# First batch's q and k loaded in rows of 2 KB and set beside each other on chip, with the planner's numbers anew

## The chip, the cores and the metric

The kernel runs on one core of a Trainium2 chip. The metric is the device time of one execution in microseconds (us); less is better. The engines named below are PE (TensorE, with its weight loads PEld), DVE (VectorE), ACT (ScalarE), POOL (GpSimd) and SP (SyncE, here the one queue that issues all DMAs).

## What is computed

Dilated and plain windowed attention over 4 batches, 8 heads, 576 tokens and 64 numbers a head, then two gated MLPs over the 2304 tokens. Cut to what matters:

```python
scores = scale * np.matmul(q, k.transpose(0, 1, 3, 2))        # q, k, v: (4, 8, 576, 64) float32
masks = [mask_plain if h < H // 2 else mask_dil for h in range(H)]   # 32 keys; or 32 keys at distance 4
attn = softmax(np.where(masks, scores, -1e9))
x = np.matmul(attn, v).transpose(0, 2, 1, 3).reshape(2304, 512)
xn = x / rms(x) * rms_g                                       # first MLP; weights are float64
x = (silu(xn @ w_gate) * (xn @ w_val)) @ w_out                # d_ff = 1536
return (sigmoid(x @ w2_gate) * (x @ w2_val)) @ w2_out         # second MLP
```

## The kernel before

**Work and order.** No engine's order is written by hand. Every piece of work is entered by `add(engine, cost, fn, reads, writes, tiles, due, other)`; `Line.emit` then runs a list scheduler that gives each engine the piece that can start first by modelled costs, ties by `due`. `other` names another engine that may take the piece, with a penalty from the table `PARAMS`. The table also holds the due times of attention groups, loads, weights and stores. What comes out is a fixed order on each of PE, DVE, ACT, POOL and SP; each engine works its list off in order, and so does SP's DMA queue.

**Attention.** Heads go in pairs `hp` (0 and 1 plain, 2 and 3 dilated), queries in blocks of 64, three blocks to a group: 4 batches x 4 pairs x 3 groups. A group (`attn_group`) is: scores on PE (L943), mask and maximum on DVE (L955), three exponentials on ACT (L961), a reciprocal on DVE (L968, L969), scaling on POOL (L974, or DVE L978, ACT L981), a transposition on PE (L988), a copy out of the bank (L993), the product with the values on PE (L1001) and a copy into the tile `xT` (L1013 or L1021).

**Loads of the first batch.** `first_qk` (L763) loads k and q of one head pair of batch 0 into a raw tile of 72 partitions: partition p holds eight tokens of both heads, token by token, so that PE can transpose both heads of a token row at once (L796, eight transpositions of 72x128, in two banks of four). Copies out of the banks (L807) put them in the order in which the attention reads them. The raw tiles lie in the rings `xo` (pairs 2 and 3), `pt` (pair 0) and `wo` (pair 1). The whole of that load is one DMA of 1152 rows of 256 bytes:

```python
raw = new(pool_, ring, [TP, 8, 2, D], F32, bufs)              # TP = 72, D = 64
out=raw.t, in_=src[b, 2*hp:2*hp+2].rearrange("e (p n) d -> p n e d", n=8)
```

Values of batch 0 come by `first_v` (dilated, tile `xT`, L855) and `values_of`. The other batches are loaded by `attn_load` (L902, rows of 128 bytes) and transposed by DVE (L916).

**MLPs.** The 2304 tokens go in six chunks of 384. `x_norm` squares x on ACT (L1051), sums on PE (L1067), takes the inverse root on DVE (chunk 0) or POOL, spreads it by PE (L1124) and writes `xn` on DVE (L1147). Every operand is split in a high and a low part by `split`: high by ACT (L582) or DVE (L584), low = source - high by POOL (L586) or DVE (L589). A step (chunk c, slice f of d_ff) is g and v (L1362, 12 matmuls each), the gate (ACT L1404, DVE L1406, L1410), the split of `h`, and one step later y (L1442, 12 matmuls). First-MLP weights are float64 bits: `words` makes float32 of one 128-row slice by ACT (L563) and four DVE instructions (L566, L569, L572, L575), behind a load of 512 KB (L542, L546) into the ring `wst` of three. The second MLP works with 2x2 block products (L1670, L1593) from about 600 us on.

## Time and profile before

| | |
|---|---|
| median of 3 runs | 1005.12 us (1004.35 to 1007.39) |
| the profiled execution | 1005.76 us, of which the span from first to last instruction is 1004.0 us |
| PE busy in the span | 974.6 us (97%), mean granted clock 0.979 |
| DVE, ACT, POOL busy | 732.4 (73%), 478.3 (48%), 405.8 (40%) us |
| DMA packets | 213252, of them 137312 under 512 B |
| DMA, mean over the span | 194 GB/s |

PE's time splits in two. From about 255 us on it is busy practically without a gap until 983 us. Before that lie the starting stage, up to the first product of the MLP, and a stage in which attention of later batches and steps of the first MLP are mixed. A stretch of the trace shows what an engine lost in two ways: as time in which it was not busy, and as granted clock below 1.00 (the clock has two levels, 1.2 and 2.4 GHz; 0.80 is a mean over the stretch). Durations given for one instruction overlap a little with the next one, so the distance between starts is the better price.

### The profile page before, as it was taken

How to read it: one execution, taken by the hardware profiler on the slowest of the kernel's cores; microseconds unless marked ns; L12 is line 12 of the kernel's file. 1: busy time of each engine (PE TensorE's matmuls, PEld its weight loads, DVE VectorE, ACT ScalarE, POOL GpSimd, SP SyncE). 2: the span in 40 equal slices, each digit the busy share in tenths (PEclk: the TensorE clock that was granted, in tenths of full speed). 3: DMA queues.
4: the chain of work that ended last, by engine and by line, in shares of the span. 5: the costliest groups of instructions: out<-in, count | busy, mean ns of one | idle time of the engine just before them, and what ended most of it. 6: DMA issues, size and time to landing. Idle time of an engine off the chain costs nothing. (4 is left out here: it accounts for less than half of the span.)

```text
span 1004.0 us, 20084 instructions
## 1 busy us (share of the span) xinstructions
PE 974.6 (97%) x7096; PEld 946.2 (94%) x7096; DVE 732.4 (73%) x1712; ACT 478.3 (48%) x1305; POOL 405.8 (40%) x602
## 2 busy tenths in 40 slices
PE   7898899999999999999999999999999999999997
PEld 6678798998999999999999999999999999999996
DVE  6787897867886888744432569778977688788766
ACT  5976657646432443222221336546654455454432
POOL 5663874443433640010000457337753037661111
PEclk8789799999999999999999999999999999999999
DMA  8858698676779687974662455545276463547634
GB/s 205 191 148 179 134 288 222 155 214 183 236 232 311 228 278 240 331 252 176 234 220 88 136 162 190 210 183 173 69 259 212 156 225 124 189 151 236 161 79 93
DMA packets 213252, 194.53 MB, mean 194 GB/s; under 512 B 137312, under 2 KB 178848, under 8 KB 213152
## 3 DMA queue, kind: packets, MB, share of 16 engines
q1 hardware_dynamic: 213152, 193.25, 63.5%
q8 instruction: 56, 0.92, 0.4%
q14 instruction: 44, 0.36, 0.1%
HBM read 129.50 MB, written 63.70 MB: 192 GB/s over the span
## 5 line engine op out<-in xcount | busy, mean ns | idle before, releaser
L1442 PE MATMUL y<-h,wo 128*128 128x384 f32 x864 | 167.9, 340 | 0.5 <-DVE h L589 0.4
L1362 PE MATMUL g<-xo,w 128*128 128x384 f32 x864 | 165.7, 340 | 0.0
L1362 PE MATMUL v<-xo,w 128*128 128x384 f32 x864 | 162.9, 336 | 0.0
L1442 PEld LDWEIGHTS y<-h,wo 128*128 128x128 f32 x864 | 150.5, 189 | 2.5 <-DVE h L589 0.7
L1362 PEld LDWEIGHTS g<-xo,w 128*128 128x128 f32 x864 | 152.2, 191 | 0.3
L1362 PEld LDWEIGHTS v<-xo,w 128*128 128x128 f32 x864 | 150.2, 188 | 1.3
L582 ACT CAST h<-t 128x384 fp32r<-128x384 f32 (+1 forms) x139 | 65.7, 473 | 111.9 <-DVE t L1410 86.3
L586 POOL TENSOR_TENSOR h<-t,h 128x288 fp32r<-128x288 f32 (+1 forms) x45 | 42.0, 934 | 156.6 <-ACT h L582 151.2
L1410 DVE TENSOR_TENSOR t<-t,v 128x384 f32<-128x384 f32 x72 | 39.6, 550 | 64.0 <-PE v L1362 63.3
L1542 DVE SCALAR_TENSOR_TENSOR pt<-y,pt 128x288 f32<-128x288 f32 x133 | 60.0, 452 | 36.0 <-PE y L1593 33.3
L974 POOL TENSOR_SCALAR pr<-pr,rs 128x96 f32<-128x96 f32 x132 | 57.1, 446 | 56.3 <-DVE rs L969 44.0
L589 DVE TENSOR_TENSOR h<-t,h 128x384 fp32r<-128x384 f32 (+1 forms) x95 | 58.5, 616 | 24.9 <-ACT h L582 23.9
L1593 PE MATMUL y<-h,wo 128*128 128x288 f32 x399 | 72.7, 295 | 0.3 <-ACT h L582 0.2
L586 POOL TENSOR_TENSOR w<-wz,w 128x256 fp32r<-128x256 f32 x58 | 47.3, 830 | 48.5 <-ACT w L582 35.2
L563 ACT ACTIVATE wz<-wst 128x512 f32<-128x512 f32 x72 | 47.9, 669 | 35.1 <-DMA z<-wz 21.7
L1593 PEld LDWEIGHTS y<-h,wo 128*128 128x128 f32 x399 | 59.5, 188 | 0.8 <-ACT h L582 0.5
L586 POOL TENSOR_TENSOR w<-S,w 128x256 fp32r<-128x256 f32 x48 | 38.7, 820 | 52.2 <-DVE w L584 38.0
L572 DVE SCALAR_TENSOR_TENSOR wz<-wst,wz 128x512 int32<-128x512 int32 x72 | 55.8, 775 | 0.9
L961 ACT ACTIVATE pr<-pr,nmx 128x96 f32<-128x96 f32 x144 | 52.4, 366 | 8.0 <-DVE nmx L955 7.7
L575 DVE SCALAR_TENSOR_TENSOR wz<-wst,wz 128x512 int32<-128x512 int32 x72 | 53.2, 738 | 0.6
L1696 ACT ACTIVATE t<-t 128x288 f32<-128x288 f32 x72 | 31.9, 444 | 45.5 <-DVE t L1687 43.9
L586 POOL TENSOR_TENSOR x<-t,x 128x288 fp32r<-128x288 f32 x29 | 27.2, 942 | 64.3 <-ACT x L582 64.3
(231 smaller groups left out, 2112.8 us busy)
## 6 DMA issues: line engine op xcount, KB each, us to landing
z<-wz SPq DMA_DIRECT2D x54, 256.0 KB, 4.7
xo<-xs SPq DMA_DIRECT2D x23, 576.0 KB, 5.7
wst<-in_moe_w_gate_dram SPq DMA_DIRECT2D x24, 512.0 KB, 4.6
wst<-in_moe_w_val_dram SPq DMA_DIRECT2D x24, 512.0 KB, 5.4
wst<-in_moe_w_out_dram SPq DMA_DIRECT2D x24, 512.0 KB, 5.4
xs<-xs SPq DMA_DIRECT2D x21, 576.0 KB, 2.8
wst<-xs SPq DMA_DIRECT2D x18, 576.0 KB, 5.3
x<-xo SPq DMA_DIRECT2D x24, 384.0 KB, 3.2
```

The source lines that it names most:

```text
L563: add("ACT", act(CW), lambda: nc.scalar.activation(out=z.t.bitcast(F32), in_=top().bitcast(F32), func=ACTF.Abs), reads=[("wst", key)], wri ...
L572: add("DVE", Shared(0.595), lambda: nc.vector.scalar_tensor_tensor(out=z.t, in0=top(), scalar=-0x40000000, in1=z.t, op0=ALU.bitwise_and, o ...
L575: add("DVE", Shared(0.595), lambda: nc.vector.scalar_tensor_tensor(out=z.t, in0=low(), scalar=29, in1=z.t, op0=ALU.logical_shift_right, op ...
L582: add("ACT", act(n), lambda: nc.scalar.copy(out=hi(), in_=src()), reads=reads, writes=[key] + [order] * bool(order), tiles=tiles + [dst], ...
L586: add("PL", pool(n), lambda: nc.gpsimd.tensor_tensor(out=lo(), in0=src(), in1=hi().bitcast(F32), op=ALU.subtract), reads=reads, writes=[ke ...
L589: other=(kind + "_lo", "DVE", dves(n), lambda: nc.vector.tensor_tensor(out=lo(), in0=src(), in1=hi().bitcast(F32), op=ALU.subtract)))
L961: add("ACT", PARAMS["exp_cost"], lambda u=u: nc.scalar.activation(out=pr.t[:, u], in_=pr.t[:, u], func=ACTF.Exp, bias=nmx.t[:, u:u + 1], s ...
L974: add("PL", Shared(0.305), lambda u=u: nc.gpsimd.tensor_scalar(out=pr.t[:, u], in0=pr.t[:, u], scalar1=rs.t[:, u:u + 1], scalar2=1.0, op0= ...
L1362: nc.tensor.matmul(out=bank.t, lhsT=w[:, l, cols], rhs=x, start=kk == order[0] and n == 0, stop=kk == order[-1] and n == 2)
L1442: nc.tensor.matmul(out=yb.t, lhsT=w.t[:, l, s], rhs=hs[r].t if broad(p, c) else hs[r].t[:, r], start=n == 0 and j == 0, stop=n == HOLDS[p] ...
L1542: add("DVE", dve(T), lambda: nc.vector.scalar_tensor_tensor(out=t.t[:, e, h], in0=bank.t, scalar=0.5, in1=t.t[:, e, h], op0=ALU.mult, op1= ...
L1593: nc.tensor.matmul(out=bank.t, lhsT=w.t[:, u, a, n], rhs=hs[u].t[:, d], start=first and u == 0 and m == 0, stop=u == NF // 2 - 1 and m == ...
```

## The change

`first_qk` gets another load. The raw tile becomes [72, 2, 8, 64]: partition p holds eight tokens of the first head, then the same eight of the second, so that a load is 144 rows of 2 KB. Two copies to a raw tile (DVE, or ACT or POOL by penalty) then lay the heads beside each other, token by token, in two tiles of the weight ring `w`, and PE transposes from these. There are 8 loads and 16 copies. All numbers of `PARAMS` that are due times or penalties differ as well.

```diff
-    "h_hi": 7.774, "h_lo": 0.002, "qk": 0.304, "norm": 0.51, "pts": 8.696, "o": 0.0, "snap": 6.738,
+    "h_hi": 1.372, "h_lo": 1.146, "qk": 0.214, "norm": 2.001, "pts": 8.071, "o": 0.332,
...
+    "turns": 2, "raw0": 0, "sign": 0, "packed": 1, "pk": 0.56, "pk_act": 0.152, "pk_pl": 0.144,
...
+        packed = PARAMS["packed"]
...
-            raw = new(pool_, ring, [TP, 8, 2, D], F32, bufs)
+            raw = new(pool_, ring, [TP, 2, 8, D] if packed else [TP, 8, 2, D], F32, bufs)
...
-                        "e (p n) d -> p n e d", n=8))
-
-            dma(load, rows(2 * S, 4 * D), writes=[("raw", nm, hk)] + ["o order"] * (ring == "wo"),
-                tiles=[raw], due=due, cost=1.1)
+                        "e (p n) d -> p e n d" if packed else "e (p n) d -> p n e d", n=8))
+
+            dma(load, rows(2 * TP, 32 * D) if packed else rows(2 * S, 4 * D),
+                writes=[("raw", nm, hk)] + ["o order"] * (ring == "wo"),
+                tiles=[raw], due=due, cost=0.5 if packed else 1.1)
+            if packed:
+                both = []
+                for a in range(2):
+                    half_ = new("sb", "w", [TP, 4, 2, D], F32, NW)
+
+                    def beside(copy, raw=raw, half_=half_, a=a):
+                        copy(out=half_.t, in_=raw.t[:, :, 4 * a:4 * a + 4].rearrange(
+                            "p e n d -> p n e d"))
+
+                    add("DVE", Shared(0.34), lambda beside=beside: beside(nc.vector.tensor_copy),
+                        reads=[("raw", nm, hk)], writes=[("raw", nm, hk, a), "wt order"],
+                        tiles=[raw, half_], due=turn_due - 1,
+                        other=[("pk_act", "ACT", 0.52, lambda beside=beside: beside(nc.scalar.copy)),
+                               ("pk_pl", "PL", pool(512), lambda beside=beside: beside(
+                                   nc.gpsimd.tensor_copy))])
+                    both.append(half_)
+                raw = both
```

The transpositions then read `raw[a]` and wait for that half alone. A third branch in `words` (`"sign"`) is added, but the table leaves it off. The line numbers of the changed program are higher: L779 becomes L797, the copies are L810, L796 becomes L834, L586 becomes L603.

**What moves, at three places.** SP's queue at the start of the program; `xo` are the raw tiles of pairs 3 and 2 (in this order), `xT` the values. Before:

```order
L546 DMA wst_288<-in_moe_w_out_dram 128x1024
L779 DMA xo_295<-in_k_dram 72x16x64
L779 DMA xo_315<-in_q_dram 72x16x64
L779 DMA xo_331<-in_k_dram 72x16x64
L779 DMA xo_337<-in_q_dram 72x16x64
L779 DMA pt_341<-in_k_dram 72x16x64
L779 DMA pt_347<-in_q_dram 72x16x64
L542 DMA wst_353<-in_moe_w_gate_dram 128x4x256
L855 DMA xT_290<-in_v_dram 64x4x64
```

and in the change:

```order
L549 DMA wst_288<-in_moe_w_out_dram 128x1024
L797 DMA xo_295<-in_k_dram 72x2x512
L797 DMA xo_307<-in_q_dram 72x2x512
L797 DMA xo_316<-in_k_dram 72x2x512
L797 DMA xo_327<-in_q_dram 72x2x512
L894 DMA xT_290<-in_v_dram 64x4x64
```

The four loads of pairs 3 and 2 stand where they stood; the values come right behind them, and pair 0 (`pt`) stands behind ten more value loads, one weight, four value loads and another weight.

ACT from its first instruction to its first exponential (`w` are the new tiles, `kT` and `qT` what the attention reads; 281 and 282 belong to pair 2, 285 and 286 to pair 3). Before:

```order
L563 ACTIVATE wz_350<-wst_288 128x512
L582 CAST w_356<-wz_335 128x256
L582 CAST w_358<-wz_335 128x256
L807 COPY kT_285<-v_366 128x288
L807 COPY kT_285<-g_373 128x288
L582 CAST w_385<-wz_344 128x256
L582 CAST w_388<-wz_344 128x256
L807 COPY qT_286<-y3_390 128x288
L807 COPY qT_286<-v_398 128x288
```

and in the change:

```order
L580 ACTIVATE wz_355<-wst_288 128x512
L810 COPY w_371<-xo_316 72x512
L810 COPY w_384<-xo_327 72x512
L846 COPY kT_281<-y3_377 128x288
L810 COPY w_397<-xo_295 72x512
L846 COPY qT_282<-g_390 128x288
L846 COPY kT_281<-v_399 128x288
L846 COPY qT_282<-y3_408 128x288
L846 COPY kT_285<-g_417 128x288
```

Four casts of weights leave this place, three of the new copies enter it, and pair 2, which is loaded third and fourth, is transposed and scored first.

POOL behind the first chunk's norm (`xo<-xn` are the low parts of x, `h` those of the gate's result). Before, where the low part of the second, third and later `h` stands on DVE:

```order
L586 TENSOR_TENSOR xo<-xn,xo 128x384
L761 MEMSET kT 128x32
L884 MEMSET v 32x128
L974 TENSOR_SCALAR pr<-pr,rs 128x96 x3
L586 TENSOR_TENSOR w<-wz,w 128x256
L974 TENSOR_SCALAR pr<-pr,rs 128x96 x3
L586 TENSOR_TENSOR w<-wz,w 128x256
L974 TENSOR_SCALAR pr<-pr,rs 128x96
L586 TENSOR_TENSOR h<-t,h 128x384
```

and in the change:

```order
L603 TENSOR_TENSOR xo<-xn,xo 128x384 x4
L603 TENSOR_TENSOR wo<-wz,wo 128x512
L1013 TENSOR_SCALAR pr<-pr,rs 128x96 x2
L603 TENSOR_TENSOR h<-t,h 128x384
L603 TENSOR_TENSOR w<-wz,w 128x256 x2
L603 TENSOR_TENSOR h<-t,h 128x384
L603 TENSOR_TENSOR w<-wz,w 128x256 x2
L1013 TENSOR_SCALAR pr<-pr,rs 128x96 x2
```

Every low part of `h` is now on POOL: all 140 of the program, where 95 were on DVE.

## Rows read from the trace of the kernel before

**Rows 1.** Engines' busy time in stretches of the first 150 us.

```profile
core 0: us, PE busy (x) PEld busy (x) DVE busy (x) ACT busy (x) POOL busy (x), PEclk, DMA share, GB/s
17.19:52.90 35.71, 31.34 (x369) 25.15 (x367) 26.50 (x135) 31.86 (x119) 20.66 (x44) 0.79 0.90 202
...
80.00:90.00 10.00, 7.47 (x53) 6.91 (x53) 9.14 (x29) 4.72 (x21) 4.15 (x7) 0.83 1.10 210
...
110.00:135.00 25.00, 21.93 (x155) 20.58 (x154) 22.97 (x59) 14.49 (x42) 23.16 (x36) 0.80 0.80 209
```

**Rows 2.** DMA over the first 30 us, in 40 slices of 0.75 us.

```profile
GB/s 0 0 2 86 285 365 385 386 400 307 205 161 162 172 155 157 124 199 109 172 185 114 198 148 280 331 255 211 184 272 305 229 188 295 277 150 180 130 113 236
```

**Rows 3.** SP's queue, first issues: start us, us, line.

```profile
2.33 0.51 SPq L546 DMA_DIRECT2D wst<-in_moe_w_out_dram  x1
2.88 1.02 SPq L779 DMA_DIRECT2D xo<-in_k_dram  x1
...
9.06 2.24 SPq L779 DMA_DIRECT2D xo<-in_q_dram  x1
```

**Rows 4.** PE in order of time, starting stage: in brackets the idle time before and its end.

```profile
10.66 0.44 PE L796 MATMUL v<-ident,xo 72*128 72x72 f32 x4 [2.60 <-DMA xo<-in_k_dram]
...
12.71 0.71 PE L796 MATMUL y<-ident,xo 72*128 72x72 f32 x4 [1.35 <-DMA xo<-in_q_dram]
...
15.50 3.38 PE L943 MATMUL att<-kT,qT 64*64 64x96 f32 x36
```

**Rows 5.** ACT in order of time, starting stage.

```profile
11.14 0.42 ACT L807 COPY kT<-v 128x288 f32<-128x288 f32 x1 [1.75 <-PE v L796]
...
17.19 0.37 ACT L961 ACTIVATE pr<-pr,nmx 128x96 f32<-128x96 f32 x1 [1.17 <-DVE nmx L955]
...
21.38 0.62 ACT L582 CAST wo<-wz 128x512 fp32r<-128x512 f32 x1
```

**Rows 6.** ACT by groups in 17.19 to 52.90 us: busy us, mean ns.

```profile
L961 ACT ACTIVATE pr<-pr,nmx 128x96 f32<-128x96 f32 x38 | 13.8, 365 | 2.5 <-DVE nmx L955 2.4
...
L563 ACT ACTIVATE wz<-wst 128x512 f32<-128x512 f32 x6 | 4.0, 669 | 0.0
...
L807 ACT COPY qT<-y 128x288 f32<-128x288 f32 x3 | 1.8, 607 | 0.0
```

**Rows 7.** What PE waited for, whole span: us, times, longest.

```profile
PE y L1001 <- DMA xT<-in_v_dram: 1.3, 3, 0.6
```

**Rows 8.** PE in order of time, first group behind the first MLP product.

```profile
63.77 1.85 PE L1362 MATMUL g<-xo,w 128*128 128x384 f32 x9
65.47 0.49 PE L988 MATMUL att<-ident,pr 128*96 128x128 f32 x3
...
67.03 0.80 PE L1362 MATMUL g<-xo,w 128*128 128x384 f32 x3
```

**Rows 9.** SP, ACT, DVE and PE from 71 to 84 us.

```profile
71.63 0.42 SPq L542 DMA_DIRECT2D wst<-in_moe_w_val_dram  x1
...
77.90 0.66 ACT L563 ACTIVATE wz<-wst 128x512 f32<-128x512 f32 x1 [5.04 <-DMA wst<-in_moe_w_val_dram]
...
79.52 1.34 DVE L589 TENSOR_TENSOR h<-t,h 128x384 fp32r<-128x384 f32 x1 [4.18 <-ACT h L582]
...
83.89 2.18 PE L943 MATMUL att<-kT,qT 64*64 64x96 f32 x24 [2.53 <-DVE qT L916]
```

**Rows 10.** The page's groups: busy us, mean ns, idle before.

```profile
L586 POOL TENSOR_TENSOR h<-t,h 128x288 fp32r<-128x288 f32 (+1 forms) x45 | 42.0, 934 | 156.6 <-ACT h L582 151.2
...
L974 POOL TENSOR_SCALAR pr<-pr,rs 128x96 f32<-128x96 f32 x132 | 57.1, 446 | 56.3 <-DVE rs L969 44.0
...
L589 DVE TENSOR_TENSOR h<-t,h 128x384 fp32r<-128x384 f32 (+1 forms) x95 | 58.5, 616 | 24.9 <-ACT h L582 23.9
```

**Rows 11.** DVE in order of time, one operation without and with POOL beside it.

```profile
7.96 0.69 DVE L575 SCALAR_TENSOR_TENSOR wz<-wst,wz 128x512 int32<-128x512 int32 x1
...
12.81 1.10 DVE L575 SCALAR_TENSOR_TENSOR wz<-wst,wz 128x512 int32<-128x512 int32 x1
```

More of the change, by code (lines that the diff above doesn't have):

```diff
@@ L19 @@
 LEAST = 2.0 ** -15
+REBIAS = 2.0 ** -112
 PARAMS = {
-    "late": 0, "fill_share": -1.519, "fill_max": 6, "gather": 0.866, "w0_hi": 17.594,
-    "w0_lo": 13.068, "h0_hi": 0.512, "h0_lo": -0.096, "x0_hi": 0.96, "x0_lo": 1.138, "ahead": 2,
-    "todo0": 464.368, "todo1": 9.635, "todo2": 47.212, "todo3": 0.618, "xb_zero": -1.082,
-    "stay": 0.104, "phase": 1.6, "fill_from": 7.028, "fill_gap": -3.039, "margin": 2139.515,
-    "wait": 1.172, "w_sq": 3.146, "w_hi": 0.024, "w_lo": 0.907, "x_hi": 0.265, "x_lo": 0.0,
@@ L45 @@
-    "rush": -0.629, "rush_to": 0.301, "raws": 1, "turns": 2, "raw0": 0,
+    "late": 0, "fill_share": -1.825, "fill_max": 6, "gather": 0.815, "w0_hi": 21.906,
+    "w0_lo": 19.193, "h0_hi": 0.957, "h0_lo": 1.801, "x0_hi": 1.843, "x0_lo": 0.685, "ahead": 2,
+    "todo0": 498.785, "todo1": 7.325, "todo2": 37.764, "todo3": -1.145, "xb_zero": -2.997,
+    "stay": 0.035, "phase": 1.6, "fill_from": 12.507, "fill_gap": -3.04, "margin": 2002.648,
+    "wait": 0.385, "w_sq": 0.927, "w_hi": 0.142, "w_lo": 0.456, "x_hi": 0.951, "x_lo": 1.674,
@@ new lines @@
+    "h_hi": 1.372, "h_lo": 1.146, "qk": 0.214, "norm": 2.001, "pts": 8.071, "o": 0.332,
+    "snap": 0.059, "h_ahead": 12.565, "h2_ahead": 3.531, "evac": 11.135, "holds": (6, 6),
+    "norm_act": 0.219, "slack": 0.0, "share_v": 0.6, "share_p": 0.33, "cold": 1.7, "low": 0,
+    "high": 0.39, "recip": 0.3, "rel1": 37.334, "span1": -1.984, "rel2": 33.192, "span2": -0.125,
+    "ys": 0.232, "ts": 0.083, "cross": 0.06, "same": 0.04, "dma_lat": 1.7, "dma_rate": 330000.0,
[3 rows of a table added]
+    "ld_b": -84.924, "ld_v": -56.098, "ld_c": -42.657, "ld_d": -6.667, "lead": 1.564,
@@ L559, in low @@
             return st.t[:, :, 0]
+        if PARAMS["sign"]:
+            add("ACT", 0.65, lambda: nc.scalar.activation(
+                out=z.t.bitcast(F32), in_=top().bitcast(F32), func=ACTF.Abs, scale=REBIAS),
+                reads=[("wst", key)], writes=[zk] + zorder, tiles=[st, z], due=due)
+            add("DVE", Shared(0.33), lambda: nc.vector.tensor_scalar(
+                out=z.t, in0=z.t, scalar1=3, scalar2=None, op0=ALU.logical_shift_left),
+                writes=[zk], tiles=[z], due=due)
+            add("DVE", Shared(0.595), lambda: nc.vector.scalar_tensor_tensor(
+                out=z.t, in0=top(), scalar=-0x80000000, in1=z.t, op0=ALU.bitwise_and,
+                op1=ALU.bitwise_or), writes=[zk], tiles=[z, st], due=due)
+            add("DVE", Shared(0.595), lambda: nc.vector.scalar_tensor_tensor(
+                out=z.t, in0=low(), scalar=29, in1=z.t, op0=ALU.logical_shift_right,
+                op1=ALU.bitwise_or), writes=[zk], tiles=[z, st], due=due)
+            return z
         add("ACT", act(CW), lambda: nc.scalar.activation(
```

29 lines of the change are left out of this document (14 added, 15 removed), and 6 rows, old and new, of the table PARAMS.

## The prediction

> **What bounds the kernel now.** I read the page first: PE is busy 97% of the span, so time is lost where PE idles or runs at the lower clock. Next come busy times by stretch, where this is seen to happen early. From 17.19 to 52.90 us ACT is the fullest engine, 31.86 of 35.71 us, with PE at a mean clock of 0.79; from 80 to 90 us PE is busy 7.47 of 10 us at 0.83; from 110 to 135 us it is busy 21.93 of 25 us at 0.80 while POOL (23.16) and DVE (22.97) are nearly full [rows 1]. The third view is the order in time of SP, PE and ACT in the starting stage. SP needs 0.51 us to issue a weight, but 1.02 to 2.24 us for a load of q or k [rows 3], and the first of these reaches PE at 10.66 us, the second at 12.71, each after a wait for the DMA [rows 4]. Scores start at 15.50 us [rows 4], the first exponential at 17.19 [rows 5], the first product of the MLP at 63.77 [rows 8]. Last I read what PE waited for around 80 us: a chain that begins at a late weight load [rows 9]. So the change touches a stage that ends with the MLP's first product; whatever makes that product earlier moves everything behind it, unless the mixed stage up to 150 us, where DVE and POOL are full, takes it back.
>
> **The loads.** A load of q or k is 2 x 576 x 64 x 4 = 294,912 bytes. While the three weights run, the DMAs move 365 to 400 GB/s; in the slices from 8.25 to 12 us, when loads of 256-byte rows run, 155 to 172 [rows 2]. At 160 GB/s a load lasts 1.84 us, at 385 GB/s 0.77. That is 1.07 us a load, and 8.6 us of DMA time for eight. Nobody waits for all of it. The first load reaches PE at 10.66 us [rows 4]; new, 9.6. In the new order scores begin with the pair that is loaded third and fourth: the fourth load lands at 9.6 + 3 x 0.77 = 11.9 us, before at 10.66 + 3 x 1.84 = 16.2. I take rows of 2 KB to run like the weights, the only loads of the trace at that time whose rows are longer; the bounds are no gain in rate (16.2) and 400 GB/s with an issue of 0.5 us (11.2).
>
> **The copies.** No row shows a copy of 72x512. On ACT the nearest is a cast of 128x512 at 0.62 us [rows 5]; on POOL a two-operand `h` of up to 384 numbers takes 0.93 [rows 10], which times 512/384 is 1.25; on DVE the two-operand integer operation on 128x512 takes 0.69 alone and 1.10 beside POOL [rows 11]. A copy beside an idle engine costs nothing. After the fourth load lands at 11.9, ACT's list has two copies and four copies out of banks before the scores, 2 x 0.62 + 4 x 0.42 [rows 5] = 2.9 us, of which one copy (of the third load) lies before 11.9; so 11.9 + 2.3 = 14.2 and the last transposition of 0.2: scores at **14.4** instead of 15.50, **-1.1 us**. Bounds: -1.8 (fourth load at 11.2) and +2 (no gain in rate: 16.2 + 1.3). The other thirteen copies lie beside PE's and ACT's work; if ACT is the limit, its one later copy is 0.62.
>
> **ACT from the first exponential to the last square of the first norm.** Counted in the two orders, ACT does in this piece two more exponentials (0.365 each), one copy (0.62), ten more small and two more large copies into `xT`, two more casts of weights; it loses five copies of kT and qT (0.607), four weight activations (0.669), two casts of 128x512 (0.62) and two small squares [rows 5, 6]. A copy into `xT` is narrower than the 288 columns that took 0.42, so I take 0.35; a cast of half the width 0.4, such a square 0.35. That is 0.7 + 0.6 + 4.2 + 0.8 = 6.3 us more and 3.0 + 2.7 + 1.2 + 0.7 = 7.6 us less: **-1.3**, as ACT is the fullest engine there (31.86 of 35.71 us [rows 1]). The bounds are 0 (another engine holds ACT up) and -2.6 (its gaps shrink as much again). In the same piece PE waited 1.3 us in three places for values of the first batch [rows 7]; these loads now stand right behind the four. ACT was busy for part of it, so I take half, **-0.6** (bounds 0 and -1.3).
>
> **What is not done yet.** Up to the MLP's first product the new order has one attention group less (16 scored instead of 17). The group costs PE 67.03 - 65.47 = **+1.6 us** later [rows 8]; the lower bound is nothing, if it fills a gap.
>
> **The late weight.** A weight is issued at 71.63 us, ACT waits for it 5.04 us, with the cast of `h` behind it in ACT's list; DVE then idles 4.18 us for that `h`, the transposition of q on DVE follows late, and PE idles 2.53 us [rows 9]. With the lower clock, (1 - 0.83) x 7.47 = 1.3 us more, 80 to 90 us cost 3.8 us [rows 1]. In the new order the weight at this place is issued behind the same stores of x and value loads, which come with the earlier start, and two weight activations that stood behind the start now stand before it. A like wait remains possible, hidden behind y of the first step. I take half: **-1.9** (bounds 0 and -3.8).
>
> **The low parts of h on POOL.** 95 of them leave DVE (0.616 each) for POOL (0.934) [rows 10]. PE needs `h` one step later, behind y and attention, so 0.3 us more are hidden while POOL is not full. Up to the second norm's low parts of x POOL gets four `h` and one sum of squares (0.93 each) and four copies (1.25) more, and seven scalings (0.446 [rows 10]) less: 4.7 + 5.0 - 3.1 = 6.6 us more. DVE, by the same counting up to the eighth step, loses six `h`, four scalings and 17 copies out of banks, and gets eight of the new copies, five of kT and qT and the four operations of one more weight. With 0.62 for `h`, 0.3 for a scaling or a narrow copy, 0.45 for a new copy (between nothing and 0.69), 0.5 for kT and 2.2 for the weight: -3.7 - 1.2 - 5.1 + 3.6 + 2.5 + 2.2 = -1.7. I set these two against each other at **0** (bounds -2 and +6.6). The later stages, where PE has no gaps, cost nothing either way; the cover is gone if POOL falls behind there.
>
> **The sum.** -1.1 - 1.3 - 0.6 + 1.6 - 1.9 = -3.3 us against the profiled execution's 1005.76 us (span 1004.0): 1002.5. That execution lies 0.6 above the median of the runs, 1005.12, so the predicted median is **1001.8 us**.
>
> **Rivals.** *The start's gain is used up in the mixed stage.* From 80 to 90 and 110 to 135 us DVE is 91 to 92% full [rows 1], and its work up to the eighth step is about the same. Then the late weight and the waits for values only change places and -1.1 - 1.3 + 1.6 = -0.8 is left: **1004.3**. For it: the full engines. Against it: DVE idled 4.18 us for a mere order of ACT's list [rows 9].
>
> *POOL becomes the bound at the second norm.* Between 110 and 135 us POOL is busy 93% [rows 1], and the norm's sums, its Newton steps and the low parts of x stand on POOL; PE's products of the second chunk wait for them. If none of the 6.6 us goes into POOL's earlier idle time, PE comes 6.6 us later, and 20% of it more is lost to the lower clock, as the mean of 0.80 in this stretch tells (1.3 us): 1001.8 + 7.9 = **1009.7**. It makes the kernel slower than before once about 3 of the 6.6 us are left over. For it: POOL slows DVE too, the same operation taking 1.10 instead of 0.69 us beside it [rows 11]. Against it: the four copies fall before 35 us, when POOL was busy about half the time (20.66 of 35.71 [rows 1]).
> The Trainium skill, page "SBUF — State Buffer", section "SBUF: two separate sides", has a sharper rule: a DVE instruction with two SBUF inputs and a GpSimd instruction that reads SBUF exclude each other for the whole instruction. By it POOL's 6.6 us would block such DVE work in full and the time would be near this rival's 1009.7. The trace agrees in part only: DVE lost 0.41 us beside POOL, whose operations last about 0.93 us each [rows 10, 11].
>
> *The loads land no earlier.* If the three weights ahead, and not the rows' size, set the pace, the copies come on top, one of 0.62 on ACT's path: **1005.7**. Against it are the slices at 155 to 172 GB/s right behind 400 [rows 2].
>
> **How the numbers follow.** About 0.3% (3.0 us) is what a measurement of this kernel can tell from no change: faster is below 1002.1, slower above 1008.1. My forecast has 0.47 (its own range 996 to 1003; I count it as faster), the used-up gain 0.22 and the unchanged loads 0.10 (same, with 0.02 of it slower for copies in the way), POOL as the bound 0.21. Faster 0.47, same 0.30, slower 0.23. All bounds on the good side would give 1005.1 - 1.8 - 2.6 - 1.3 - 3.8 - 2 = 993.6; with a tenth left out below and a tenth above, the range is 994.5 to 1010.
>
> **What the profile would show.** Right: the four q and k loads issued in 0.5 us each, transpositions before 12 us, scores near 14.4, first MLP product near 62 with ACT still fullest before it, no ACT wait of 5 us for a weight between 70 and 80, and PE busy at least as much as before in 100 to 150. Wrong: scores at 15.5 or later (loads or copies); scores early but the first MLP product at 64 or later (ACT, or casts of weights left undone); an early product, but PE waiting for POOL's low parts or sums between 100 and 140; gaps after 300 us, where POOL now has every low part of `h`.

## The result, and the profile after

The change takes 1014.82 us (median of 4 runs, 1012.86 to 1016.42) against 1004.99 before: a ratio of 1.0101, 95% interval 1.0076 to 1.0125. It is about 10 us slower, where 3.3 us less were forecast, and lies above the range. The profiled execution has a span of 1014.5 us (before 1004.0).

The first view is again that of busy times by stretch, now of the change, for the stretches of [rows 1] and, last, from its first exponential to the last square of the first norm:

```profile
core 0: us, PE busy (x) PEld busy (x) DVE busy (x) ACT busy (x) POOL busy (x), PEclk, DMA share, GB/s
17.19:52.90 35.71, 33.15 (x358) 25.65 (x356) 23.23 (x122) 28.79 (x117) 19.39 (x47) 0.74 0.80 158
80.00:90.00 10.00, 8.42 (x90) 7.00 (x84) 7.50 (x33) 8.11 (x28) 4.91 (x7) 1.00 0.94 218
110.00:135.00 25.00, 20.20 (x143) 19.18 (x143) 22.47 (x54) 16.08 (x53) 20.89 (x31) 0.73 0.65 151
...
19.55:56.02 36.47, 33.91 (x377) 26.29 (x375) 22.59 (x120) 30.12 (x124) 19.57 (x49) 0.73 0.72 140
```

In the first stretch PE is now the fullest engine, 33.15 of 35.71 us, at a lower mean clock (0.74, before 0.79), and ACT has lost 3 us of work. From 80 to 90 us things are better than before; from 110 to 135 us PE does less at a lower clock, though POOL is less busy than it was.

Two numbers of such a row make PE's loss: the time in which it was not busy, and the busy time times (1 - clock). Taken over the whole span they give a simple account. Before: 29.4 us idle, 19.1 lost to the clock, and 955.5 of work at full clock. The change: 36.8, 22.5 and 955.2. These are estimates, worked out from the mean clock of each stretch. By them the work is about the same; the 10.5 us of span are 7.4 more of idle time and 3.4 more of clock. By stage, idle and clock together, in us (the columns behind the third are experiments, told below):

| stretch | before | change | change again | old order, copies | new order, no copies | told only | narrow turns |
|---|---|---|---|---|---|---|---|
| 0 to 17 | 7.1 | 9.4 | 9.4 | 8.5 | 8.9 | 8.3 | 5.0 |
| 17 to 50 | 9.8 | 9.9 | 10.0 | 15.6 | 10.7 | 13.4 | 8.6 |
| 50 to 70 | 5.3 | 11.7 | 12.5 | 8.1 | 12.1 | 8.9 | 5.4 |
| 70 to 100 | 4.2 | 2.7 | 2.3 | 3.5 | 3.3 | 4.4 | 1.0 |
| 100 to 150 | 9.2 | 12.4 | 11.0 | 9.3 | 10.5 | 14.4 | 8.8 |
| 150 to 260 | 4.1 | 0.5 | 0.5 | 1.0 | 0.6 | 0.5 | 0.6 |
| 260 to 980 | 1.1 | 5.3 | 3.1 | 1.1 | 4.2 | 2.6 | 2.5 |

So the change loses 2.3 us at the start, 6.4 at the first norm, 3.2 in the mixed stage and 4.2 late, and wins back 1.5 and 3.6. Each column is one profiled execution, and the column "change again" shows how far two executions of one kernel differ.

The start, in the DMA slices of 0.75 us [rows 2]:

```profile
GB/s 0 0 2 56 255 380 366 411 401 382 226 228 212 212 220 240 197 174 168 152 149 117 120 229 362 192 166 284 380 223 194 233 198 191 152 174 186 225 235 269
```

SP's queue in order of time [rows 3]:

```profile
2.88 0.45 SPq L797 DMA_DIRECT2D xo<-in_k_dram  x1
...
4.20 0.46 SPq L797 DMA_DIRECT2D xo<-in_q_dram  x1
4.71 10.75 SPq L894 DMA_DIRECT2D xT<-in_v_dram  x10
```

PE in order of time, at the start and at the first norm [rows 4, 8]:

```profile
13.40 0.71 PE L834 MATMUL y<-ident,w 72*128 72x72 f32 x4 [5.92 <-POOL w L810]
14.79 0.74 PE L834 MATMUL g<-ident,w 72*128 72x72 f32 x4 [0.68 <-ACT w L810]
...
17.86 2.18 PE L982 MATMUL att<-kT,qT 64*64 64x96 f32 x24
...
61.99 0.90 PE L1163 MATMUL y<-ident,rb 128*128 128x128 f32 x3 [3.20 <-DVE rb L1147]
...
65.48 0.91 PE L1040 MATMUL att<-pts,v 96*64 96x64 f32 x12 [1.11 <-ACT pts L1032]
...
67.47 2.00 PE L1401 MATMUL g<-xo,w 128*128 128x384 f32 x6
```

ACT in order of time [rows 5, 9]:

```profile
12.68 0.62 ACT L810 COPY w<-xo 72x512 f32<-72x512 f32 x1 [3.54 <-DMA xo<-in_k_dram]
14.12 0.62 ACT L810 COPY w<-xo 72x512 f32<-72x512 f32 x1 [0.82 <-DMA xo<-in_q_dram]
...
62.65 0.66 ACT L580 ACTIVATE wz<-wst 128x512 f32<-128x512 f32 x1 [1.41 <-DMA wst<-in_moe_w_val_dram]
```

The issues are short, as forecast, but the data come late: behind the weights the slices show 212 to 240 GB/s. Pair 2, scored first, is loaded third and fourth; its k lands at 12.68 us, its q at 14.12, scores start at 17.86 (before 15.50), the MLP's first product at 67.47 (63.77). At the first norm PE has run out of attention and waits 3.20 us for DVE's root, then for ACT, which stands before a weight whose load came late. Before, PE waited 1.56 us for that root:

```profile
58.15 0.55 PE L1124 MATMUL y<-ident,rb 128*128 128x128 f32 x3 [1.56 <-DVE rb L1108]
```

The root itself took longer in the change. Two of its steps, which take 0.16 us each elsewhere in it and in the kernel before, took 0.58 and 0.65 us. First these steps on DVE, then what POOL did meanwhile, two low parts of a weight:

```profile
59.89 0.58 DVE L1131 TENSOR_TENSOR rsa<-rsy 128x3 f32<-128x3 f32 x1
60.51 0.65 DVE L1132 SCALAR_TENSOR_TENSOR rsa<-rsa,ms 128x3 f32<-128x3 f32 x1
```

```profile
59.69 1.44 POOL L603 TENSOR_TENSOR w<-wz,w 128x256 fp32r<-128x256 f32 x2 [1.37 <-ACT w L599]
```

Each of the two steps ends within 0.03 us of one of POOL's two instructions. They make 0.9 us of the 1.64 by which PE's wait grew.

The copies on POOL and DVE, in order of time, are cheaper than the nearest rows suggested:

```profile
12.71 1.16 POOL L810 COPY w<-xo 72x512 f32<-72x512 f32 x2 [5.97 <-DMA xo<-in_k_dram]
```

```profile
14.12 1.10 DVE L810 COPY w<-xo 72x512 f32<-72x512 f32 x3 [2.36 <-DMA xo<-in_q_dram]
```

### The profile page after: what moved, and what is told of

Its sections match the earlier page's. It is cut to its first block, busy times and chain, and to the rows that moved or that the text cites. A ratio compares the mean times of both kernels' runs of the same rounds, so it can differ in the third digit from the quotient of the medians.

```text
span 1014.5 us, 20150 instructions
## 1 busy us (share of the span) xinstructions
PE 977.7 (96%) x7096; PEld 946.6 (93%) x7096; DVE 678.3 (67%) x1548; ACT 489.7 (48%) x1358; POOL 547.8 (54%) x729
## 4 chain that ended last, share of the span: by engine, by line
PE 80%; DMA 7%; DVE 5%; POOL 2%; SPq 2%; ACT 2%; issue 1%; DVEq 0%; ACTq 0%; POOLq 0%
PE g L1401 14%; PE v L1401 13%; PE y L1481 13%; PE y L1632 12%; PE att L1709 10%; PE v L1709 4%; PE y L1709 4%; PE g L1709 4%; DMA wz<-z 2%; PE att L982 2%; DMA wst<-in_moe_w_out_dram 1%; PE att L1040 1%; DMA xo<-in_q_dram 1%; PE att L1027 1%; DMA op<-pt 1%
## 5 line engine op out<-in xcount | busy, mean ns | idle before, releaser
L603 POOL TENSOR_TENSOR h<-t,h 128x384 fp32r<-128x384 f32 (+1 forms) x140 | 137.4, 983 | 194.1 <-ACT h L599 192.2
L1013 POOL TENSOR_SCALAR pr<-pr,rs 128x96 f32<-128x96 f32 x115 | 49.1, 441 | 45.1 <-DVE rs L1008 21.7
L603 POOL TENSOR_TENSOR x<-t,x 128x288 fp32r<-128x288 f32 x43 | 37.4, 872 | 44.3 <-ACT x L599 44.2
L1270 DVE TENSOR_TENSOR t<-t,t 128x288 f32<-128x288 f32 x67 | 50.2, 749 | 16.5 <-POOL h L603 6.5
L592 DVE SCALAR_TENSOR_TENSOR wz<-wst,wz 128x512 int32<-128x512 int32 x72 | 59.2, 823 | 0.8
L583 DVE TENSOR_SCALAR wz<-wz 128x512 f32<-128x512 f32 x72 | 45.0, 627 | 20.7 <-ACT wz L580 20.2
L589 DVE SCALAR_TENSOR_TENSOR wz<-wst,wz 128x512 int32<-128x512 int32 x72 | 58.2, 809 | 1.0
L1726 DVE TENSOR_TENSOR t<-t,att 128x288 f32<-128x288 f32 x96 | 42.0, 447 | 20.5 <-PE att L1709 19.1
```

Source lines behind the costliest of these rows:

```text
L589: add("DVE", Shared(0.595), lambda: nc.vector.scalar_tensor_tensor(out=z.t, in0=top(), scalar=-0x40000000, in1=z.t, op0=ALU.bitwise_and, o ...
L592: add("DVE", Shared(0.595), lambda: nc.vector.scalar_tensor_tensor(out=z.t, in0=low(), scalar=29, in1=z.t, op0=ALU.logical_shift_right, op ...
L603: add("PL", pool(n), lambda: nc.gpsimd.tensor_tensor(out=lo(), in0=src(), in1=hi().bitcast(F32), op=ALU.subtract), reads=reads, writes=[ke ...
L1013: add("PL", Shared(0.305), lambda u=u: nc.gpsimd.tensor_scalar(out=pr.t[:, u], in0=pr.t[:, u], scalar1=rs.t[:, u:u + 1], scalar2=1.0, op0= ...
L1270: add("DVE", dves(n), lambda: nc.vector.tensor_tensor(out=dst(), in0=a(), in1=c(), op=ALU.subtract), reads=reads, writes=writes, tiles=til ...
```

## The experiments

Three theories stood against each other. P: the packed load and its copies cost the time. T: the new numbers of the planner cost it. R: the other order that the planner made costs it, whatever led the planner to it. To keep them apart, some kernels don't plan at all: the order of a program, operation by operation and with its engines, is written down and replayed, so that one thing can be changed and nothing else moves.

**Packing under the old numbers.** The change with the table of the kernel before:

```diff
-    "h_hi": 1.372, "h_lo": 1.146, "qk": 0.214, "norm": 2.001, "pts": 8.071, "o": 0.332,
+    "h_hi": 7.774, "h_lo": 0.002, "qk": 0.304, "norm": 0.51, "pts": 8.696, "o": 0.0, "snap": 6.738,
...
```

> The changed kernel with the due times and penalties of the kernel before: loads in rows of 2 KB, sixteen copies, nothing else. Theory T (the new numbers cost the 10 us: later start because values go ahead of pair 0 and between, POOL's low parts of h, a late weight in the second MLP): 1002 to 1006. Theory P (the load and its copies cost it: copies between landing and transposition, PE idle and at the low clock behind it): 1010 to 1016, scores at 17 us or later. Both say nothing exact of the mixed stage, since the scheduler places everything anew.

Measured: 1017.88 us, ratio 1.0131 (1.0104 to 1.0157); scores at 18.56 us. That is above both ranges; the late scores are as theory P said, and theory T fails here.

**The new numbers without packing.**

```diff
-    "turns": 2, "raw0": 0, "sign": 0, "packed": 1, "pk": 0.56, "pk_act": 0.152, "pk_pl": 0.144,
+    "turns": 2, "raw0": 0, "sign": 0, "packed": 0, "pk": 0.56, "pk_act": 0.152, "pk_pl": 0.144,
```

> The changed kernel with its new numbers, but the loads in rows of 256 bytes and no copies. Theory T (the new numbers cost it): 1012 to 1018, and a delay of 3 us or more in the second MLP as in the change. Theory P (the load and its copies cost it): 1002 to 1006, scores at 15 to 16 us.

Measured: 1013.93, ratio 1.0098 (1.0067 to 1.0129). Theory T had this one right, and P fails. Each half alone is about as slow as the whole; by P one of the two had to be fast, by T the other. Either half makes the planner place everything anew, so the next runs hold the order fixed.

**The old order with rows of 2 KB and copies.** The list scheduler gives way to a recorded list, and the copies get the ring of h:

```diff
     def emit(self):
...
+        for word in plan:
+            n, eng, fills = word.split(",")
...
+                    half_ = new("sb", "h", [TP, 4, 2, D], F32, 2)
```

> The kernel before with its recorded order replayed on every engine, loads in rows of 2 KB, and the sixteen copies put in right ahead of their transpositions (two on ACT, four on DVE, ten on POOL), into the ring of h, which is empty then. Theory R (copies and rows cost next to nothing, the 10 us are what the planner's other order costs): 1002 to 1006. Theory P (copies on the way between landing and transposition cost it): 1010 or more.

Measured: 1008.76, ratio 1.0037 (1.0010 to 1.0064), between the two expectations. My placing put copies behind other work (a copy on POOL took 1.07 us between low parts of weights), scores start at 17.78 us, and 17 to 50 us loses 15.6 us, mostly to the clock. So the 0.4% holds what my placing cost, too.

**The new order without rows of 2 KB and copies**, replayed in the same way with `packed` at 0:

> The changed kernel's recorded order replayed on every engine, but loads in rows of 256 bytes and the sixteen copies left out. Theory R: the order alone costs it, 1012 to 1018, with the same gaps in the second MLP near 600 and 770 us. Theory P: 1003 to 1008.

Measured: 1018.65, ratio 1.0140 (1.0102 to 1.0178), just above the range of theory R and far from that of P. With the order fixed, packing makes -0.4% in the new order (1.0101 against 1.0140, not clear of noise, as the intervals overlap) and +0.4% in the old; the new order makes +1.4% without packing and +0.6% with it.

**The planner told, nothing else changed.** The kernel before, whose planner believes that the loads are cheap:

```diff
-            dma(load, rows(2 * S, 4 * D), writes=[("raw", nm, hk)] + ["o order"] * (ring == "wo"),
-                tiles=[raw], due=due, cost=1.1)
+            dma(load, rows(2 * TP, 32 * D), writes=[("raw", nm, hk)] + ["o order"] * (ring == "wo"),
+                tiles=[raw], due=due, cost=0.5)
```

> The kernel before, with no operation changed: only the planner is told that the eight loads cost SP 0.5 us and the bus less, so it places the work anew. If another order by itself costs what the change lost: 1008 to 1018. If the planner's orders are worth about the same: 1003 to 1007.

Measured: 1017.74, ratio 1.0143 (1.0114 to 1.0172). The same operations on the same data, placed anew, cost as much as the change. It loses elsewhere (13.4 us from 17 to 50, 14.4 from 100 to 150): not one late step but a worse order at several places. With the run before, this decides for R: another order alone costs it.

**Rows of 2 KB alone.** The kernel before, its order kept:

```diff
-                    out=raw.t, in_=src[b, 2 * hp:2 * hp + 2].rearrange(
-                        "e (p n) d -> p n e d", n=8))
+                    out=raw.t.rearrange("p n e d -> p (n e d)").rearrange("p (e x) -> p e x", e=2),
+                    in_=src[b, 2 * hp:2 * hp + 2].rearrange("e (p n) d -> p e (n d)", n=8))
```

> The kernel before with one thing changed: the eight loads of q and k of batch 0 bring rows of 2 KB into the same raw tile. No copy is added and PE transposes what lies there, so the reordering of the tokens is left out and the attention of batch 0 is not the reference's; the order on every engine is that of the kernel before, instruction by instruction. Theory A (rows of 2 KB run near 385 GB/s; in the change they were late because the value loads of 256-byte rows, issued 4.7 us in, shared the DMAs with them): here no value load stands between, so the first load reaches PE at 9.0 to 9.8 us (before 10.66), the second by 10.7 (12.71), the slices behind the weights show 300 GB/s or more, scores start 1.5 to 3 us earlier. Theory B (a load on 72 partitions runs at about 220 GB/s whatever stands beside it): the slices stay at 200 to 240, the first load arrives at 10.0 to 10.5, the second at 11.5 to 12, scores start about 1 us earlier. Time: 1002 to 1005 by both, since the order behind is fixed and only waits shift.

Measured: 1003.00, ratio 0.9985 (0.9966 to 1.0004). Its DMA slices:

```profile
GB/s 0 0 1 63 279 369 376 386 365 380 216 178 221 210 249 281 253 251 215 183 218 210 243 255 237 232 244 214 233 94 165 379 264 167 147 215 245 144 219 248
```

With no value load between, the slices behind the weights still show 178 to 221 GB/s, as theory B said, though some lie below its 200. The second load came at 11.65 us, scores at 14.24.

> The kernel before with rows of 2 KB on partitions 0 to 71 and no copies, once more beside it: 180 to 250 GB/s behind the weights, the second load at 11.5 to 12 us, ratio 0.997 to 1.000.

Measured: 1000.91, ratio 0.9975 (0.9955 to 0.9995); second load at 10.75 us, ahead of what was expected. The same program lands 0.9 us earlier in another execution.

**Where the data go.** The same bytes on partitions 0 to 35 and 64 to 99:

```diff
-                nc.sync.dma_start(
+                nc.sync.dma_start(out=raw.t[0:36], in_=tokens[0:36])
+                nc.sync.dma_start(out=raw.t[64:100], in_=tokens[36:72])
```

> The kernel before, its order kept, with loads in rows of 2 KB as two DMAs of 36 partitions each, into partitions 0 to 35 and 64 to 99. The first half of the transpositions reads the one, the second half the other; heads and tokens are not put in order, so the attention of batch 0 is not the reference's. Theory S (72 neighbouring partitions reach only part of the ways into SBUF, as the Trainium skill has it, page SBUF — State Buffer, section on the DMA port swizzle: partitions 0 to 63 share eight of sixteen ports): the slices behind the weights show 270 GB/s or more, the second load reaches PE by 10.9 us (11.65 with 72 partitions). Theory L (the rows' length or the count of 72 sets it): 180 to 250 GB/s as before, the second load at 11.5 to 12. The time: 1000 to 1005 by both.

Measured: 1004.26, ratio 1.0004 (0.9985 to 1.0024), and in the slices:

```profile
GB/s 0 0 2 56 194 382 386 392 404 366 216 210 219 221 224 221 224 247 272 205 255 200 278 262 243 234 169 283 200 209 267 352 127 197 72 200 268 203 188 268
```

Still 210 to 224 GB/s in the slices behind the weights, so the mark of 270 GB/s is missed. The other mark of theory S is met, the second load comes at 10.46 us; but the run above has 10.75 without spreading, so it tells nothing. The Trainium skill, page "SBUF — State Buffer", section "Door 1: The DMA port swizzle", says that a DMA's bandwidth depends on how many of sixteen ports its partitions reach. Here each half is a DMA of its own, on 36 neighbouring partitions, so no DMA was spread, and the run doesn't test that rule: whether it sets the rate stays open.

**The pair that is scored first, loaded first.** The new order replayed, four loads of SP exchanged, here in words:

```text
before the edit: k of pair 3, q of pair 3, k of pair 2, q of pair 2
behind it:       k of pair 2, q of pair 2, k of pair 3, q of pair 3
```

> The changed kernel's recorded order with one exchange on SP: the loads of pair 2, which is transposed first, go out ahead of those of pair 3. If PE's wait of 5.92 us at the start is the wait for the third load in a queue that moves some 220 GB/s, the first copy starts at 10.0 to 10.4 us (12.68), scores at 15 to 15.6 (17.86). By a theory that a late start moves everything behind it, the time falls by as much, to 1012 to 1013; by theory R (the mixed stage and the second MLP decide) by 1 us or less.

Measured: 1017.23, ratio 1.0121 (1.0086 to 1.0157). Scores start at 15.96 us, 1.9 earlier, and nothing is won; the time lies above both expectations. The rows show where the 1.9 us went, though not why:

```profile
12.00:24.00 12.00, 11.53 (x104) 9.65 (x105) 6.43 (x41) 7.50 (x29) 3.94 (x9) 0.50 0.87 204
28.00:44.00 16.00, 15.75 (x148) 13.58 (x148) 9.12 (x43) 12.78 (x48) 7.48 (x18) 0.50 0.72 128
```

PE is busy almost throughout, but at the clock 0.50 in both stretches (in the change 9.81 us at 0.62 and 14.42 at 0.79); the clock costs 19.7 us from 17 to 70 us, where the change lost 14.7.

**Zeros in the wait at the start**, in that kernel:

```diff
+                def turn(src=src, n0=n0, bank=bank, wait=19 * ((nm, hp, a) == ("k", 2, 0))):
+                    filler(bank)[0](wait)
                     for r in range(4):
```

> The changed kernel's recorded order, the loads of pair 2 first as in the experiment before, and 19 products of zeros on PE while it waits for the first copy (7.3 to 10.8 us); they add nothing to the output. Theory C (the earlier start was eaten by the lower clock, which stayed at 0.50 from 12 to 24 and from 28 to 44 us): the clock is 1.00 up to the scores at least, scores start at 14.8 to 15.6 (15.96), the loss to the clock from 17 to 70 us falls from 19.7 to 10 to 15 us, and the time to 1007 to 1013. Theory D (the order sets it, the clock only follows): clock 0.50 again behind 20 us, time 1015 to 1018.

Measured: 1013.54, ratio 1.0103 (1.0066 to 1.0140); the row of the first stretch below has 1.00, the next one 0.50.

```profile
8.00:14.00 6.00, 3.64 (x35) 3.29 (x33) 4.44 (x9) 2.36 (x5) 0.92 (x2) 1.00 0.88 199
15.00:24.00 9.00, 9.00 (x89) 7.57 (x91) 5.53 (x37) 5.75 (x25) 3.31 (x8) 0.50 0.78 207
```

Theory C misses its marks: the clock is 1.00 to about 14 us and not up to the scores, these start at 16.48 us, and the clock's loss from 17 to 70 us is 16.3 us. The time lies just above C's range and below D's, and the intervals of the two kernels overlap. What the low clock cost here is left open.

**Zeros at the first norm too:**

```diff
+            filler(rbp)[0](9 * (not c))
             for t in range(TT):
```

> The kernel of the run with 19 products of zeros at the start (changed order, pair 2 first), and 9 more ahead of the first norm's transposition, where PE waited 3.36 us for DVE's Newton steps at the clock 0.50. They add nothing to the output. Theory C (the low clock costs the time there): the clock is 1.00 within 4 us behind the wait, the first product of the MLP comes at 65 to 67 us (68.51) and the time falls by 1 to 3 us. Theory D (the order costs it: behind the wait PE waits for ACT and POOL anyhow): the first product at 68 or later, the time the same within 1 us.

Measured: 1015.06, ratio 1.0117 (1.0089 to 1.0146). PE in order of time:

```profile
59.24 2.51 PE L832 MATMUL y<-zeros 128*128 128x288 f32 x9
62.81 0.55 PE L1229 MATMUL y<-ident,rb 128*128 128x128 f32 x3 [1.05 <-DVE rb L1212]
...
67.18 0.91 PE L1105 MATMUL att<-pts,v 96*64 96x64 f32 x12 [3.00 <-ACT pts L1097]
```

and what ACT did in that wait:

```profile
64.35 0.67 ACT L643 ACTIVATE wz<-wst 128x512 f32<-128x512 f32 x1 [2.28 <-DMA wst<-in_moe_w_val_dram]
```

The products behind the root now take 0.55 and not 0.90 us, so the clock is up, and PE then waits 3.00 us for ACT, which waits for a weight. The first product comes at 69.18 (68.51 without these zeros), as theory D said, and theory C fails: the time is no lower. So in the stretch behind the root the order costs the time, and a higher clock only lengthens a wait. From 48 to 60 us and from 68 to 72 the clock stays at 0.50, and of these the run says nothing.

**The low parts of h back on DVE:**

```diff
-    "h_hi": 1.372, "h_lo": 1.146,
+    "h_hi": 7.774, "h_lo": 0.002,
```

> The changed kernel with two numbers of the kernel before, the penalties of the high and the low part of h, so that DVE takes most low parts of h again. If POOL's 95 low parts of h are what costs time (the rival of the prediction), 3 to 8 us come back, most of it between 100 and 140 us: 1007 to 1012. If the start and the late weights cost it, no more than 2 us either way: 1013 to 1017.

Measured: 1014.76, ratio 1.0099 (1.0063 to 1.0135). On POOL 62 are left instead of 140, and the time is the same. The planner placed everything anew for it, so the run doesn't show what these 78 operations alone are worth. The rows of the page, the change's first, then this kernel's:

```profile
L603 POOL TENSOR_TENSOR h<-t,h 128x384 fp32r<-128x384 f32 (+1 forms) x140 | 137.4, 983 | 194.1 <-ACT h L599 192.2
```

```profile
L603 POOL TENSOR_TENSOR h<-t,h 128x384 fp32r<-128x384 f32 (+1 forms) x62 | 63.0, 1016 | 108.2 <-ACT h L599 106.9
```

**The gap in the second MLP.** In the profiled execution PE waited 2.53 us at 770 us, behind DVE, which stood 4.47 us before a sum of weight blocks. The order replayed, with that sum six operations later on DVE and its two successors on POOL behind one low part of h; DVE's part of the list, in short:

```text
moved from here: TENSOR_TENSOR S<-wz 128x256
                 TENSOR_TENSOR t<-t,g 128x288
...
                 SCALAR_TENSOR_TENSOR pt<-y,pt 128x288
to here:         TENSOR_TENSOR S<-wz 128x256
```

> The changed kernel's recorded order with one exchange in the second MLP: DVE's sum of two weight blocks that waited 4.47 us for a DMA at 769 us stands six instructions later, behind the work of the running step, and its two successors on POOL behind one low part of h. If the late weight in front of DVE's list is the whole of PE's gap there (2.5 and 0.3 us), 2 to 3 us come back: 1011 to 1013.5. If PE or DVE would have waited for that weight anyhow: within 1 us of 1014.8.

Measured: 1017.81, ratio 1.0138 (1.0108 to 1.0168). The gap is gone (0.41 us idle from 600 to 800 us, before the edit 3.94), the time is not, and it fits neither expectation: its profiled execution loses 4.07 us from 800 to 980 and is later from the start on.

> The changed kernel itself, beside the others: ratio 1.008 to 1.013 as before. If its ratio here is above 1.012, the runs with pair 2 first and with the weight behind were no slower than it.

Measured: 1013.73, ratio 1.0110 (1.0083 to 1.0138). The same stretch, in the first execution of the change and in this one:

```profile
600.00:800.00 200.00, 196.06 (x1468) 194.81 (x1468) 143.35 (x267) 111.38 (x295) 144.36 (x156) 1.00 0.50 180
```

```profile
600.00:800.00 200.00, 199.47 (x1496) 198.83 (x1497) 145.61 (x273) 111.28 (x295) 143.77 (x157) 1.00 0.50 179
```

So the gap of 3.9 us is of one execution, not of the kernel. What repeats is the start and the first norm, and in part the mixed stage (11.0 us, first 12.4) and the late loss (3.1, first 5.3; table above). The runs with pair 2 first and with the weight behind were no faster than the change.

**Rows of 2 KB without copies, complete.** PE transposes each head by itself, in the old order:

```diff
-                    for r in range(4):
+                    for r, e in [(r, e) for r in range(4) for e in range(2)]:
 
-                        nc.tensor.transpose(
-                            bank.t[:, r], raw.t[:, 4 * a + r].rearrange("p e d -> p (e d)"),
-                            ident[0:TP, 0:TP])
+                        nc.tensor.matmul(
+                            out=bank.t[64 * e:64 * e + 64, r], lhsT=raw.t[:, e, 4 * a + r],
+                            rhs=ident[0:TP, 0:TP], start=True, stop=True)
```

> The kernel before, its order on every engine kept instruction by instruction, with the loads in rows of 2 KB and no copy: PE transposes each head by itself, two products of 72x64 against the identity (the second into partitions 64 to 127 of the bank) in the place of one transposition of 72x128. The output is complete. If the earlier landing seen without any reordering (second load 1.1 us earlier, scores 1.26 us earlier) is the whole gain to be had and 128 narrow products cost no more than PE's waits for loads: 1001 to 1004. If the doubled products on PE cost their full length (16 more groups of 0.4 to 0.7 us, half of them beside busy stages): 1006 to 1010.

Measured: 1002.64, ratio 0.9983 (0.9963 to 1.0003). PE in order of time:

```profile
9.94 0.72 PE L796 MATMUL v<-ident,xo 72*64 72x72 f32 x16 [1.65 <-DMA xo<-in_k_dram]
```

The row holds one bank: eight narrow products, for each of which the trace has two records. They take 0.72 us where the four transpositions of a bank took 0.44 [rows 4]. The doubling is not free: over the first 50 us PE's work on the line that transposes is, before and then in this kernel,

```profile
0.00:50.00 50.00, 7.60 (x64) 6.37 (x64) 0.83 0.87 198
0.00:50.00 50.00, 12.63 (x256) 11.10 (x256) 0.83 0.85 200
```

5.0 us more at the same mean clock. The time is no longer all the same, as the wait before the first load lands has shrunk from 2.60 to 1.65 us and the scores start at 14.96 us, 0.5 earlier. The stage table counts these products as work and not as loss.

With 10 products of zeros in the first wait:

```diff
+                def turn(raw=raw, a=a, bank=bank, wait=10 * ((nm, hp, a) == ("k", 3, 0))):
+                    filler(bank)[0](wait)
+                    for r, e in [(r, e) for r in range(4) for e in range(2)]:
```

> The kernel with rows of 2 KB, the order of the kernel before and two narrow products for each transposition, and 10 products of zeros on PE in its wait for the first load (8 to 9.9 us). Theory C: the clock, which there stayed at 0.50 from 14 to 26 us, is 1.00 for most of it, scores start at 13.6 to 14.4 (14.96), and the time is 998 to 1002. Theory D: 1002 to 1004, since ACT sets the pace behind the scores.

Measured: 1001.62, ratio 0.9979 (0.9961 to 0.9997); the clock stays at 1.00 up to 26 us, yet scores start at 14.89 and the ratio is about that of the kernel without zeros (0.9983), where 14 to 26 us were at 0.50. So the clock of that stretch is worth nothing here, as theory D had it for the time. With 8 more at the first norm:

```diff
+            filler(rbp)[0](8 * (not c))
             for t in range(TT):
```

> The kernel with narrow transpositions and 10 products of zeros at the start, and 8 more in its wait for the first norm (1.56 us). Theory C: no stretch at 0.50 from 56 to 61 us, first product of the MLP at 59 to 59.8 us (60.47), time 0.5 to 1.5 us below that kernel, ratio to before 0.9965 or less. Theory D: the same as that kernel within 0.5 us.

Measured: 1002.83, ratio 0.9987 (0.9967 to 1.0007). The clock is 1.00 from 56 to 61 us, but the first product of the MLP comes at 65.23 us and the time is no lower: theory C fails here too.

The last run splits each load of the narrow kernel into 64 and 8 partitions:

```diff
+                nc.sync.dma_start(out=raw.t[0:64], in_=tokens[0:64])
+                nc.sync.dma_start(out=raw.t[64:72], in_=tokens[64:72])
```

> The kernel with rows of 2 KB, the order of the kernel before and two narrow products for each transposition, each load as two DMAs, of 64 partitions and of 8; the output is complete. Theory K (a load is shared out over as many of the 16 DMA engines as divide its partitions, so 72 and 36 partitions use fewer than 64 or 128; the Trainium skill has such a rule on page DMA: Bandwidth & Descriptors): the slices behind the weights show 270 GB/s or more, and scores start 0.5 us or more ahead of 14.96. Theory L (something else in these loads, not the count): 200 to 250 GB/s, scores at 14.5 to 15.5. The time: 1000 to 1003 by theory K, 1001 to 1004 by L.

Measured: 1001.16, ratio 0.9945 (0.9925 to 0.9964), the lowest ratio of all, but neither theory's marks are met: the slices behind the weights show 139 to 224 GB/s, and scores start at 16.69 us.

```profile
GB/s 0 0 0 82 302 378 392 370 363 377 153 139 205 224 205 219 183 240 158 227 193 191 221 256 285 182 140 252 309 225 202 187 300 241 119 190 91 157 197 226
```

Its ratio is low because the kernel before took 1005.80 us beside this run (1002.89 to 1005.15 beside the others); its own time is within 0.2% of its three relatives'. These have ratios of 0.9979 to 0.9987, two of them with an interval that reaches 1, so this form is no slower than the kernel before and perhaps 0.1 to 0.2% faster, or 0.5% by the last run; it beats the change by over 1%. The Trainium skill, page "DMA: Bandwidth & Descriptors", section "Why a DMA increments its semaphore by 16 and not by 1", has the rule that a load uses as many of sixteen DMA engines as divide its partitions. The trace agrees as far as the engines go: from 7.5 to 12 us they are busier than in the run with two loads of 36 partitions (DMA share 1.07 against 0.81), but they move less (191 GB/s against 219), so the count of engines bought no rate here.

## Why the prediction was wrong

**The loads (forecast -1.1, measured +2.4 at the scores).** This step failed at its rate. I took loads in rows of 2 KB to run like the weights, at 385 GB/s and 0.77 us a load; they ran at 212 to 240, with no value load between at 178 to 238, and the third and fourth landed 1.44 us apart. The fourth load came at 14.12 us, not at 11.9, within the bound (16.2). SP's issues did get shorter (0.35 to 0.46 us), and the rate rose from 155 to 172 by some 40%, but it did not double. The scores at 17.86 are even past the bound of +2: PE's and ACT's steps behind the landing took 3.7 us where 2.5 were forecast, with PE at 0.50. The bound itself was worked out wrongly, with 1.3 us behind the landing where the forecast has 2.5; with 2.5 it is +3.2, and the measured +2.4 lies within. The rival that loads land no earlier is not what happened: at the old rate the fourth load would land at 16.2.

**The copies.** Sound, and too dear on POOL: about 0.6 us in three of four (0.87 in one) instead of 1.25; 0.62 on ACT; on DVE about 0.4.

**ACT up to the last square (forecast -1.3).** ACT's work fell as counted: from the first exponential, 19.55 us, to the last square it is busy 30.12 us instead of 31.86. But the stretch is 36.47 us instead of 35.71, +0.8 us: ACT was no longer the fullest engine. PE was, busy 33.91 us of it at the clock 0.73, and that PE bounds it is read from this fullness, not tried. The step took the fullest engine of the old order to be the fullest of the new.

**The waits for values (-0.6).** The mechanism held: PE's waits in the change name no DMA any more, where before there were 1.3 us in three places. What that was worth in time no run shows.

**The group put off (+1.6)** had the right sign, and not its place. The rows suggest that PE lacked this work during the first norm's root, where it stands for 3.20 us instead of 1.56; no run tried it, and 0.9 us of the difference is the root's two steps beside POOL (above). The prediction priced the group where it is done and not where it is missing; 50 to 70 us loses 6.4 us more.

**The late weight (-1.9).** 80 to 90 us lost 3.8 us and now loses 1.6: right in kind. But another weight holds ACT up to 62.65 us, behind the first norm's root, where PE waits for ACT.

**POOL.** The rival had its place right (100 to 150 us loses 3.2 more in one execution, 1.8 in the other), and its cause is not borne out: with the low parts of h back on DVE nothing is won, though in a kernel that was planned anew. What the trace does show is POOL beside DVE at the first norm's root, by low parts of weights and not of h. There a step of 0.16 us took 0.58 and another 0.65, each to the end of a POOL instruction. This agrees with the sharper rule that the prediction named from the Trainium skill, page "SBUF — State Buffer", section "SBUF: two separate sides". The prediction took the 0.41 us that DVE lost [rows 11] for agreement in part only; but that DVE operation began in the midst of a POOL instruction that ran from 12.23 to 13.36 us, so by that rule it could lose no more than the 0.55 us that were left of it.

**What the sum left out.** This is the step that failed most. Behind each of its terms stood the belief that the new order is as good as the old one wherever I did not look, so everything else was put at nothing. The new order alone, without rows of 2 KB and copies, costs 1.4%; the run in which the planner alone was told something else costs as much without a changed operation. A rival of that kind (the order placed anew is worse at places nobody can name) was missing, and it was what happened. Every kernel of this record that was planned anew (the change, the old table, the one without packing, the one with h back, the one that was only told) costs 1.0 to 1.4%, so the order of the kernel before was a better one than the planner comes to by the way; why is open. Which places of the order cost how much is read from the stage table and not shown one by one: the two repairs of single places, pair 2 first and the weight behind, won nothing.

## What to carry to other kernels

Where a planner places the work, first replay the recorded order with the one change in it; a kernel that is planned anew measures the new order, here up to 1.4%, and the change under test is a fraction of that. Count work that is moved away also at the place where it may have covered a wait, and not only where it lands. And take a load's rate from a load of the same shape: weights with rows of 1 and 4 KB to 128 partitions, at 385 GB/s, said nothing of rows of 2 KB to 72.

## What was not expected of the hardware

Loads to 72, 36 and 64 partitions with rows of 2 KB ran at 140 to 240 GB/s behind weights at 365 to 411; why is left open. The DMA engines' busy share rose from 0.81 to 1.07 with loads of 64 and 8 partitions and the bytes did not; one DMA spread over far partitions was not tried. Steps of 0.16 us on DVE took 0.58 and 0.65 us beside POOL, on a path for which PE waited. An earlier start can win nothing: scores 1.9 us earlier, then PE at 0.50 from 12 to 24 and 28 to 44 us, and the time no better; that the clock is the reason is not shown, as in the kernel with narrow products the clock of the start was worth nothing. And the landing of the same loads differs by 0.9 us between executions of one program.
